# Cross-attention and a snake MoE on one core: steps in an order made offline with a PSUM bank each, the first input in quarters, 64-wide transposes, squares on three engines, slice pairs

## The chip, the cores and the metric

One core of one Trainium2 chip runs the whole program. The metric is the device time of an execution in microseconds (us); a median over several executions is quoted, and the comparisons use runs of the same state (fast). The profile is one execution; its span, from the first to the last instruction, is 1.7 to 2.1 us shorter than the time of the same execution in the thirteen runs where both are on record.

## The reference, cut to what matters

```python
# x (8, 8, 512, 64), state (8, 8, 32, 64); w_in (512, 2048), w_out (2048, 512), alpha (2048)
scores = scale * x @ state.T              # per batch and head: 512 x 32
xread  = softmax(scores) @ state          # 512 token rows
sread  = softmax(scores.T) @ x            # 32 state rows
x2     = concat([xread, sread])           # heads side by side: 8 * 544 rows of 512
h      = x2 @ w_in
g      = h + sin(alpha * h)**2 / (alpha + 1e-9)
out    = g @ w_out                        # 4352 rows of 512, fp32
```

Both kernels fold the state into w_in: M = state @ w_in for each batch, so that h of the token rows is A @ M, with A the normalized weights. The 256 state rows of all batches are done last ("batch 8" below).

## The kernel before

A loop over batches t and over 16 feature blocks f. In each pass it gives a matmul pair for h, some steps of the next batch's attention by a table of slots, the snake (sine, square, gT) two blocks later, and a few output matmuls of the batch before. PSUM has three pools: 4 banks for h, 2 for outputs, 2 for all else.

```python
nc.sync.dma_start(st_nat[:], state...)                 # 512 KB, first in the queue
for k in range(G): nc.sync.dma_start(x_first[...], ...) # batch 0's x in two halves
...
nc.gpsimd.tensor_copy(held[:], st_nat[:, 0, 0:1])      # the weight loads wait for the state
...                                                    # then w_in and w_out by GpSimd's queue

def m_step(b, fs, on_act):                             # one slice of 512 columns of M
    mp = [psX.tile(...) for _ in range(G)]
    for h in range(2):
        for g in range(G):
            for r in range(2):                         # 8 matmuls of 64 rows x 32 columns
                nc.tensor.matmul(mp[g][o0:o0 + Ns, :], stT[rows, ...], w_in_sb[rows, ...])

if f in PLAN[kind(t)]["sq"]: late.append((s2, s, n))   # square on VectorE, one pass later
else: nc.gpsimd.tensor_tensor(s2, s, s, ALU.mult)      # or on GpSimd

# state rows, at the very end: a store writes 4 batches x 32 rows
eng.dma_start(ov[st * n:(st + 1) * n, S:, cols], o_sb[:, cols])
```

The last 128 state rows are two halves of 256 columns, each with its own copy and store.

The softmax here doesn't subtract the row's maximum and nothing guards it: scores larger than these inputs give would overflow.

## Time and profile before

| | |
|---|---|
| time, median of 3 | 240.83 us (239.0 to 241.3) |
| span in the profile | 237.7 us |
| first h matmul, first output matmul | 15.98 us, 25.42 us |
| last matmul ends, tail after it | 230.51 us, 7.2 us |
| busy: TensorE, ScalarE, VectorE, GpSimd | 219.4, 176.9, 171.6, 99.0 us |

How to read it: the span is the start up to the first h matmul, then TensorE's own work with whatever it idles, then the tail. From 61 us on TensorE has no gap of note. Only three things can shorten the span: an earlier start, less idle time or less work between the first h and the last matmul, and a shorter tail. The prediction shows the lines for each.

### The profile page before, as it was taken

To read this page: it belongs to the slowest core of one execution; us is meant where nothing else is said; L and a number is where in the kernel's file an instruction comes from. 1 tells how busy PE (TensorE), PEld (TensorE's weight loads), DVE (VectorE), ACT (ScalarE), POOL (GpSimd) and SP (SyncE) were. 2 spreads that over 40 slices of the span, in tenths; PEclk is the share of its full clock that TensorE was granted. 3 is DMA by queue.
4 is the path that set the end of the run, shared out by engine and by line. 5 is a ranking of instruction groups with operands and counts; after the bars stand their busy time and mean duration, and the time that the engine had idled before them with its cause. 6 is when DMAs were issued, how large, how long until landed. Compare 5 with 4: busy or idle time off the path is not lost.

```text
span 237.7 us, 4198 instructions
## 1 busy us (share of the span) xinstructions
PE 219.4 (92%) x1532; PEld 104.1 (44%) x1532; DVE 171.6 (72%) x321; ACT 176.9 (74%) x277; POOL 99.0 (42%) x107
## 2 busy tenths in 40 slices
PE   6785699898999999999999999999999999999970
PEld 1643233433444344434443444344434444566550
DVE  3569798789878986898689868985889776645300
ACT  3588777889899979997999799969997565554310
POOL 2946494078543354335433544333433356201100
PEclk9999999999999999999999999999999999999997
DMA  6999993913661556075605560540141111111211
GB/s 217 171 196 206 205 156 91 173 48 72 97 148 36 136 97 130 31 138 100 127 31 140 98 126 29 141 112 4 42 132 47 44 45 45 47 44 48 89 21 67
DMA packets 36578, 23.35 MB, mean 98 GB/s; under 512 B 19645, under 2 KB 32205, under 8 KB 36557
## 3 DMA queue, kind: packets, MB, share of 16 engines
q0 software_dynamic: 11504, 7.87, 23.2%
q1 hardware_dynamic: 25020, 15.21, 22.1%
q8 instruction: 12, 0.20, 0.3%
q14 instruction: 10, 0.07, 0.1%
q10 hardware_dynamic: 32, 0.01, 0.1%
HBM read 17.31 MB, written 8.91 MB: 110 GB/s over the span
## 4 chain that ended last, share of the span: by engine, by line
PE 79%; DMA 8%; POOL 4%; issue 2%; ACT 2%; DVE 2%; POOLq 0%
PE o_ps L415 47%; PE h_ps L380 20%; DMA w_out_sb<-in_moe_w_out_dram 6%; PE m_ps L361 4%; PE h_ps L386 3%; DMA st_nat<-in_state_dram 2%; POOL s L396 2%; PE o_ps L440 1%; PE w_ps L316 1%; POOL w_in_sb L159 1%; PE s_ps L271 1%; PE w_ps L327 1%; DVE gT L406 1%; ACT s L391 1%; ACT o_sb L421 0%
## 5 line engine op out<-in xcount | busy, mean ns | idle before, releaser
L415 PE MATMUL o_ps<-w_out_sb,gT 128*128 128x512 bf16 x528 | 135.5, 380 | 2.4 <-DMA w_out_sb<-in_moe_w_out_dram 1.9
L391 ACT ACTIVATE s<-h_ps,alpha_sb 128x512 bf16<-128x512 f32 (+1 forms) x144 | 95.0, 674 | 36.8 <-PE h_ps L380 26.3
L396 POOL TENSOR_TENSOR s<-s 128x512 bf16<-128x512 bf16 (+1 forms) x70 | 71.0, 1021 | 102.0 <-ACT s L391 98.2
L406 DVE SCALAR_TENSOR_TENSOR gT<-s,inva_sb,h_ps 128x512 bf16<-128x512 bf16 (+1 forms) x144 | 98.7, 706 | 15.1 <-POOL s L396 14.3
L380 PE MATMUL h_ps<-AT,M 128*128 128x512 bf16 x256 | 75.5, 379 | 1.9 <-DVE gT L406 1.0
L415 PEld LDWEIGHTS <-gT 128*128 128x128 bf16 x528 | 49.2, 98 | 59.8 <-issue 8.4
L380 PEld LDWEIGHTS <-M 128*128 128x128 bf16 x256 | 24.3, 98 | 31.0 <-issue 4.8
L403 DVE TENSOR_TENSOR s<-s 128x512 bf16<-128x512 bf16 (+1 forms) x74 | 29.0, 411 | 8.5 <-ACT s L391 8.2
L370 ACT CAST M<-m_ps 128x512 bf16<-128x512 f32 x49 | 27.1, 598 | 0.0
L421 ACT COPY o_sb<-o_ps 128x512 f32<-128x512 f32 x33 | 19.3, 588 | 6.1 <-PE o_ps L415 5.1
L284 DVE TENSOR_REDUCE R<-E 128x16 f32<-128x512 bf16 x16 | 10.9, 683 | 14.9 <-ACT E L280 14.9
L280 ACT ACT_TABLE_LOAD x12 | 15.4, 1283 | 0.2
L391 ACT ACT_TABLE_LOAD x12 | 15.4, 1283 | 0.2
L361 PE MATMUL m_ps<-w_in_sb,stT 64*32 64x512 bf16 x256 | 13.7, 393 | 0.2 <-ACT M L370 0.2
L295 POOL TENSOR_TENSOR A<-E,rR 128x512 bf16<-128x512 bf16 x7 | 7.3, 1046 | 15.8 <-DVE rR L285 15.8
L372 DVE CAST M<-m_ps 128x512 bf16<-128x512 f32 x15 | 10.3, 687 | 4.2 <-PE m_ps L361 4.2
L280 ACT ACTIVATE E<-s_ps 128x512 bf16<-128x512 f32 x16 | 9.4, 597 | 3.3 <-PE s_ps L271 3.2
L361 PEld LDWEIGHTS <-stT 64*32 64x32 bf16 x256 | 3.9, 89 | 13.7 <-issue 13.6
L386 PE MATMUL h_ps<-xs_all,w_in_sb 128*128 128x256 bf16 x64 | 9.6, 273 | 0.0
L386 PEld LDWEIGHTS <-w_in_sb 128*128 128x128 bf16 x64 | 6.3, 98 | 4.1
L271 PEld LDWEIGHTS <-xT 128*128 128x128 bf16 x128 | 5.9, 101 | 4.9 <-DVE xT L249 1.8
L336 DVE RECIPROCAL rC<-w_ps 128x128 f32<-128x128 f32 x8 | 7.6, 944 | 0.6 <-PE w_ps L327 0.6
(53 smaller groups left out, 101.0 us busy)
## 6 DMA issues: line engine op xcount, KB each, us to landing
out_dram<-o_sb SPq DMA_DIRECT2D x33, 256.0 KB, 2.3
xnat<-in_x_dram POOLq DMA_DIRECT2D x7, 512.0 KB, 6.8
w_in_sb<-in_moe_w_in_dram POOLq DMA_DIRECT2D x4, 512.0 KB, 9.5
w_out_sb<-in_moe_w_out_dram POOLq DMA_DIRECT2D x4, 512.0 KB, 18.1
x_first<-in_x_dram SPq DMA_DIRECT2D x2, 512.0 KB, 6.2
st_nat<-in_state_dram SPq DMA_DIRECT2D x1, 512.0 KB
out_dram<-o_sb SPq DMA_DIRECT2D x2, 128.0 KB
xT<-xp SPq DMA_TRANSPOSE x6, 3.8
```

The lines of the kernel that those rows point to most:

```text
L280: nc.scalar.activation(a.E[:, g], a.sp[g][:], ACT.Exp, scale=scale)
L284: nc.vector.reduce_sum(a.R[:, g], E8, axis=AX.X)
L361: nc.tensor.matmul(mp[g][o0:o0 + Ns, :], stT[rows, b * G + g, c0:c0 + Ns], w_in_sb[rows, 2 * g + h, fs * FW:(fs + 1) * FW], start=True, st ...
L370: nc.scalar.copy(dst, mp[g][:])
L380: nc.tensor.matmul(hp[:, :n], Ms[t][:, g, f * P:(f + 1) * P], atts[t].AT[:, g, :], start=(g == 0), stop=(g == G - 1),)
L386: nc.tensor.matmul(hp[:, :n], w_in_sb[:, q, f * P:(f + 1) * P], xs_all[:, q, :], start=(q == 0), stop=(q == Q - 1),)
L391: nc.scalar.activation(s[:, :n], hp[:, :n], ACT.Sin, scale=alpha_sb[:, f:f + 1])
L396: nc.gpsimd.tensor_tensor(s2[:, :n], s[:, :n], s[:, :n], ALU.mult)
L403: nc.vector.tensor_tensor(s2[:, :n], s[:, :n], s[:, :n], ALU.mult)
L406: nc.vector.scalar_tensor_tensor(gT[t][:, f, :n], s2[:, :n], inva_sb[:, f:f + 1], hp[:, :n], ALU.mult, ALU.add)
L415: nc.tensor.matmul(op[:], gT[t][:, ft, st * P:(st + 1) * P], w_out_sb[:, ft, :], start=(ft == 0), stop=(ft == FT - 1),)
L421: nc.scalar.copy(o_sb[:], op[:])
```

## The change

The loop and the slot tables are gone. One list of 1336 steps, made offline, gives the program order of everything; each step that needs PSUM names its bank. With it come other changes: batch 0's x in four quarters on two queues and no gate ahead of the weight loads; batch 0's state as a load of its own; transposes that read two heads side by side, 64 columns wide, without a packed copy; squares on GpSimd, ScalarE or VectorE by name; both exp of a batch nearly always side by side; two slices of M in one step from batch 2 on; batch 1's transpose of A by DMA; and another end.

```diff
-PLAN = {0: {'P': (0, 1), ... }}                     # slots by batch and block
+ORDER = """
+lq.0.A lq.1.S consts lq.2.A l_st0 zero.0 ident_ warm_up.6.512.0 zero.1 exp_table lq.3.S l_st
+identf.V li.0 l_alpha xq.0.V li.1 xtq.0.1 xq.1.A li.3 ...
+...                                                 # [cut: some 120 lines]
+""".split()
-    psH = ... bufs=4 ...; psO = ... bufs=2 ...; psX = ... bufs=2 ...
+        k.gpool, k.sinp, k.outp = pool("gpool", 38), pool("sinp", 10), pool("outp", 6)
+        k.banks = [pool(f"bank{i}", 1, space=bass.MemoryType.PSUM) for i in range(8)]
-    held = const.tile([P, 1], FP32, name="held")
-    nc.gpsimd.tensor_copy(held[:], st_nat[:, 0, 0:1])
+    def xt(k, b, g, bank):                           # 64-wide, straight from the load
+        ... k.nc.tensor.transpose(tp[k.half(r), h, ...], k.t["xnat", b][:, 2 * (2 * g + h) + r, ...], ...)
+    def m(k, b, s, *banks):                          # 2 banks: one slice, 4 banks: two
+        for n in range(len(banks) // 2): ...
+    def sq(k, t, f, eng):
+        if eng == "A": k.nc.scalar.activation(s2[:, :n], s[:, :n], ACT.Square)
+        else: k.mul(eng, s2[:, :n], s[:, :n], s[:, :n])
-            eng.dma_start(ov[st * n:(st + 1) * n, S:, cols], o_sb[:, cols])
+            k.nc.sync.dma_start(ov[:, k.S + st::2, cols], o_sb[:, cols])   # 8 batches x 16 rows
+    for step in ORDER:
+        name, *args = step.split(".")
+        getattr(steps, name)(*(int(a) if a.isdigit() else a for a in args))
```

In the list, `h.0.12.2` is h of batch 0, block 12, in bank 2; `si`, `sq`, `gt` are its sine, square and snake; `o.t.st.f0.f1` are output matmuls, `oc` and `os` their copy and store. At the end, the state rows' outputs now come before the last token rows of batch 7.

## The prediction

> **What bounds the kernel now.** I read the page's slices first, then the chain that ended last, then the table of stretches, then the timeline of TensorE, and last the groups by shape for the durations. The slices:
>
> ```profile
> PE   6785699898999999999999999999999999999970
> DVE  3569798789878986898689868985889776645300
> ACT  3588777889899979997999799969997565554310
> GB/s 217 171 196 206 205 156 91 173 48 72 97 148 36 136 97 130 31 138 100 127 31 140 98 126 29 141 112 4 42 132 47 44 45 45 47 44 48 89 21 67
> ```
>
> A slice is 5.9 us. TensorE is full from the eleventh slice to the last but one; before that it is at 5 to 9 tenths, and the bytes are at their highest in the first six slices. The stretches say the same in microseconds:
>
> ```profile
> 18.00:24.00 6.00, 3.16 (x38) 1.74 (x36) 5.87 (x11) 5.14 (x8) 3.52 (x4) 1.00 1.24 206
> 24.00:30.00 6.00, 4.05 (x30) 1.42 (x30) 4.41 (x9) 4.39 (x8) 3.09 (x3) 1.00 1.24 204
> 80.00:100.00 20.00, 20.00 (x145) 9.16 (x144) 15.99 (x31) 17.66 (x27) 8.79 (x9) 1.00 0.46 93
> ```
>
> The columns are TensorE, its weight loads, VectorE, ScalarE and GpSimd in us, then clock, DMA share and GB/s. From 80 to 100 us TensorE never rests, while ScalarE has 2.3 us to spare in 20. From 18 to 24 it rests for 2.8 us of 6.
>
> The chain that ended last, in order of time, at its start and its end:
>
> ```profile
> 0.74 4.39 DMA st_nat<-in_state_dram
> 10.01 15.36 DMA w_out_sb<-in_moe_w_out_dram
> 25.42 1.02 PE o_ps L415 x4
> ...
> 222.69 4.32 PE o_ps L415 x20
> 227.00 3.51 PE o_ps L440 x32
> ```
>
> The state's load gates all weight loads (a GpSimd copy of it stands before them), the first slice of w_out lands at 25.4, and only then can output matmuls start. The last two lines give rates: 4.32/20 = 0.216 us for 512 columns, 3.51/32 = 0.110 for 256. TensorE's last matmul ends at 230.51; the span is 237.7, so the tail (copy, store, end) is 7.2. The first h matmul starts at 15.98 (timeline). Between lie 214.5 us.
>
> How much of that is work? 528 output matmuls x 0.2155 = 113.8; 32 halves x 0.110 = 3.5; 256 h x 0.2155 = 55.2; 64 h of the state rows x 0.1085 = 6.9 (four of them take 0.43 between neighbours). The M step is read here:
>
> ```profile
> 121.52 0.59 PE L380 MATMUL h_ps<-AT,M 128*128 128x512 bf16 x2
> 122.04 0.41 PE L361 MATMUL m_ps<-w_in_sb,stT 64*32 64x512 bf16 x8
> 122.38 1.25 PE L415 MATMUL o_ps<-w_out_sb,gT 128*128 128x512 bf16 x5
> ```
>
> From 121.52 to 122.38 is 0.86; two h matmuls are 0.43, so a slice costs 0.43, twice its 0.215 of streaming. After the first h there are 31 slices = 13.3. Scores 14 x 0.24 = 3.4, the W product 7 x 0.46 = 3.2, the column sums 7 x 0.35 = 2.5 (from starts at 113 to 134 us), transposes of batch 1 about 1.4. Sum 203.2. So 11.3 us of 214.5 are idle, nearly all before 61 us; the chain there runs over the w_out load, gT, ScalarE copies and, from 51 to 60 us, GpSimd squares.
>
> **What the Trainium skill says.** (1) "TensorE: Matmul & The Clock Gate", section "Wait — 56ns, not 53.3ns?": 215.7 ns start to start for 512 columns when warm. The trace agrees (0.216), so this rate can't be improved by an order. (2) "TensorEngine Tiling (Array Packing)", section "Key Properties": changing the tiling mode drains TensorE. The trace agrees: 0.215 beyond streaming per M slice, entered and left from full-array matmuls. (3) "ScalarE: Activation LUTs", section "What ACT_TABLE_LOAD costs": a load is about 1283 ns, an ACTIVATE with immediates 186 ns + 0.833 per element, and neighbours overlap by about 93 ns. The trace has
>
> ```profile
> L391 ACT ACTIVATE s<-h_ps,alpha_sb 128x512 bf16<-128x512 f32 x128 | 87.4, 699 | 27.1 <-PE h_ps L380 26.3 <-POOL A L292 0.2
> L391 ACT ACT_TABLE_LOAD x12 | 15.4, 1283 | 0.2
> L280 ACT ACT_TABLE_LOAD x12 | 15.4, 1283 | 0.2
> ```
>
> and three sines in a row took 1.87, so 0.62 each. The overlap is real, about 0.075. (4) "DMA: Bandwidth & Descriptors", section "Queues, rings and completion order": each DMA engine goes round the queues that have work, packet by packet. No wait of this trace tests it; I use it for the x quarters below.
>
> **The change part by part.** No useful matmul is removed; the order, the banks and the loads change.
>
> Start. The state's load no longer stands before x and the weights. Batch 0's x comes as four 256 KB quarters on two queues, batch 0's state separately as 64 KB, all states in bf16 through GpSimd's queue, which is not gated any more. Before, 1.5 MB were landed at about 8 us (the x cast started at 8.14 without a wait). x and the small state are 1.1 MB; with part of the bandwidth going to the ungated loads I put the last quarter at 6.5. From there, by the order's text and measured durations: cast 0.45, transposes 0.25, copy 0.57, scores 0.3, two exp 1.2 (in part before the last scores), row sums, reciprocals and the normalization on VectorE up to 5.3 after landing, transpose and copy, while ScalarE does sine table 1.5, three stT copies 1.75 and two M copies 1.1. I reach 7.0 after landing, so the first h at 13.5 in place of 16.0: gain 2.5.
>
> Weights. To the first w_out slice GpSimd's queue now reads 0.5 (state) + 3 (w_in) + 1 (x of batch 1) + 1 (w_out) MB, with 1.1 MB on the others: 6.9 MB in 10^6 bytes. Before, 6.3 MB (four w_in, x, one w_out) took from about 6.7 to 25.4: 336 GB/s. At that rate it lands at about 22.5, 3 us earlier. In front of the first output matmuls the new order has 7.8 us of TensorE work (11 h pairs, 4 M slices, the 64-wide transposes), where the old had 4.4 from first h to first output. In the same stretch ScalarE has 9.8 us, or 9.0 with overlap. So idle to the first output, at about 22.8, is near 1.5 in place of 5.0.
>
> Slice pairs. 12 pairs (batches 2 to 7) drain once for two slices: estimate 0.215 + 2 x 0.215 = 0.645 in place of 0.86; 12 x 0.215 = 2.6 saved, all on the path, since TensorE is full there.
>
> 64-wide transposes. They transpose two heads side by side without the packed copy before them and drop the state's doubling (one VectorE and one ScalarE cast, 0.69 and 1.04). TensorE pays about 1.3 for batch 1 in place of 0.9; the wait on the pack before the old transpose (1.44) goes, counted in the idle time. Batch 1's second transpose goes to DMA: 0.5 less on TensorE.
>
> Work after the first h, new: 179.4 (outputs and h) + 6 single slices 2.6 + 12 pairs 7.7 + scores 3.4 + W 3.7 + sums 2.8 + transposes 1.3 = 200.9.
>
> Engines. Squares: 88 GpSimd, 49 ScalarE, 7 VectorE, before 70 and 74 on GpSimd and VectorE. A square on ScalarE is an estimate by the skill's rule: 186 + 427 = 0.61. Counting the order: 49 squares 27.5 on ScalarE; M copies 34 (before 49) and output copies 23 (before 33, and one half) give back about 15; table loads fall from 26 to 16, giving 12.8. So ScalarE stays near 177 busy. From the first h to the scores of batch 5 the sums are TensorE 98.6, ScalarE 104.8 as rows, about 95 with overlap, VectorE 96, GpSimd 63. TensorE still leads, by little. In the last third it leads by 15 and more.
>
> Sum: 13.5 + 200.9 + idle + tail. I allow 5 idle: 1.5 to the first output, 1 to 1.5 up to batch 2's scores (TensorE 20.3, ScalarE 21.2 as rows, VectorE 20.5), 2 in the rest. Tail 7.5: the last copy is whole (0.59 for 0.42) and its store 256 KB, not 128. Span 226.9. The kernel before took 240.83 for a span of 237.7, so 3.1 on top: 230.0. Since an order found offline would close such gaps where it can, I go to 229.5.
>
> **The rivals.** (a) ScalarE becomes the bound. Its stretch to batch 5 is 104.8 without overlap against 98.6; were that the truth, 6 us more idle: about 234. For it: 17.66 busy in 20 even now, and squares come on top in the middle. Against: 10 fewer table loads, overlap seen. (b) Ungated loads slow the x quarters, and the weights still arrive at their own rate: the start gains nothing, +2.5, about 232. For it: the DMA's share is already 0.94 to 1.31 in the first 30 us. (c) The fixed order meets other latencies than it was made for (DMA transposes take 3.8 and 2.7 us, loads up to 18), and a bank held by one late copy stops TensorE, whose queue is in program order: idle stays at 10, about 234 to 237. For it: the chain at 51 to 60 us shows how one late square stalls all; against: 38 gT buffers and 10 for squares leave room. (d) Square on ScalarE needs another table: 49 x one to two loads of 1.28 = 63 to 126 us slower. The page on ScalarE does not say that Square is in the sine's set, but copies between sines reload nothing here; 2 in 100.
>
> **Range and chances.** Zero idle would give 225, idle as before 235.5 or so. 80%: 225 to 235. Faster by over 2% means under 236.0: 0.89; within 2% (rival c in full, or a and b together): 0.08; slower 0.03.
>
> **What would show it.** The first h near 13.5, the first output matmul at 22 to 24; M groups of 16 in a row with 0.64 between their neighbours; 16 table loads; TensorE full from about 40 us; ScalarE busy near 177 and squares of 0.61 there without loads; the last matmul at 218 to 221. Wrong if TensorE shows idle before waits on ScalarE after 60 us (a), the last x cast starts after 8 us (b), or long waits on one bank's copy or a DMA transpose fill the middle (c).

## The result, and the profile after

The changed kernel takes **228.44 us** (228.19 to 228.61, 4 runs) against 240.7 in the same rounds. The ratio is 0.9507, with a 95% interval of 0.9465 to 0.9549. Ratios here are the mean time of one kernel's fast runs over that of the other's fast runs of the same rounds, so not quite the ratio of the medians. The prediction said 229.5 and 225 to 235. The time fell by 12.3 us, the span of the two profiled executions by 11.0: in later rounds, executions of the kernel before with the profiled span (237.6 to 237.8) took 239.6 to 239.8 us, so the profiled one was quicker than the median. All executions of that kernel in later rounds had a mean granted clock of 0.958 to 0.994, the four of the changed kernel 1.0. What follows explains the 11.0.

The slices of the changed kernel (a slice is 5.7 us):

```profile
PE   4599899999999899999999999989999999999993
DVE  3268997998897958888898888798368558782000
ACT  3299988998899899889997599799573789981122
GB/s 175 213 202 206 206 174 55 174 189 123 19 62 127 171 64 0 196 140 85 35 58 229 145 50 0 130 193 5 46 0 154 36 46 49 46 48 3 94 83 102
```

TensorE stands at 8 or 9 tenths from the third slice to the last but one, where before that took until the sixth. But the first two slices are emptier than before: 4 and 5 tenths for 6 and 7. And the last slice has work in it where there was none. The chain of the changed kernel, in order of time, at the start (start, duration, what):

```profile
1.76 8.32 DMA x<-in_x_dram
10.10 0.43 DVE xp L321
...
16.61 1.56 ACT M L467 x3
...
25.38 0.70 DVE gT L514
26.08 0.04 issue
26.12 0.59 PE o_ps L525 x2
```

The last quarter of x, issued at 1.76, takes 8.3 us. The first h matmul, before and after:

```profile
15.98 0.59 PE L380 MATMUL h_ps<-AT,M 128*128 128x512 bf16 x2 [0.72 <-ACT AT L310]
```

```profile
17.25 0.88 PE L484 MATMUL h_ps<-AT,M 128*128 128x512 bf16 x2 [0.21 <-ACT M L467]
```

The first output matmul is at 26.12, after 25.42 before. So the start has become later, not earlier, by 1.3 us. Yet the span is 11.0 shorter. Of the stretch from the first outputs to 61 us this is the line of before and then the line of the changed kernel (TensorE, its weight loads, VectorE, ScalarE, GpSimd busy us with counts, then the clock granted to TensorE as a share of full speed, the busy share of the DMA engines, GB/s):

```profile
25.40:61.30 35.90, 33.39 (x244) 13.52 (x244) 30.90 (x54) 29.03 (x48) 22.18 (x22) 1.00 0.68 125
```

```profile
26.00:61.00 35.00, 34.30 (x221) 15.16 (x225) 31.74 (x55) 31.69 (x50) 21.04 (x21) 1.00 0.72 133
```

Idle time fell from 2.5 to 0.7 us here. (Busy counts a matmul's modelled end too, so true idle is larger in both.) From 60 to 100 us, in the changed kernel:

```profile
60.00:100.00 40.00, 38.86 (x284) 18.14 (x288) 33.40 (x55) 37.06 (x57) 20.16 (x20) 1.00 0.51 106
```

The kernel before had 39.90 busy there. The new order idles for 1.1 us there where the old one idled for 0.1, and it fills the gaps that the old one had early. ScalarE is busy for 93% of this stretch.

The parts of the two spans, by the timeline of TensorE and the counts of the prediction:

| part | before | predicted | measured |
|---|---|---|---|
| start, up to the first h | 15.98 | 13.5 | 17.25 |
| work from there | 203.2 | 200.9 | 200.9 by count |
| idle between | 11.3 | 5 | 4.8 = 222.96 - 17.25 - 200.9 |
| tail after the last matmul | 7.2 | 7.5 | 3.75 = 226.7 - 222.96 |
| span | 237.7 | 226.9 | 226.7 |

The chain at the end of the changed kernel, where the last output matmuls end at 222.96 and the last copy follows:

```profile
220.63 2.34 PE o_ps L525 x10
222.99 0.58 ACT o_sb L533
```

Eleven us are: 1.3 lost at the start, 6.5 won in idle time, 2.3 in work, 3.5 in the tail. Work is counted, so idle time is a remainder and takes up any error of the count. TensorE's busy time in the same two stretches (207.7 of 214.5 us, 201.3 of 205.7) would leave 6.8 and 4.5 us idle, because each matmul before a short gap is drawn longer than its 0.216 us. How the 8.8 us of both terms divide is therefore an estimate. The predicted time is near the measured one because two terms were off by the same 3.75 us in opposite directions. The experiments take these up one by one.

### The profile page after: what moved, and what is told of

Same layout as the page of the kernel before. It is cut to its first block, busy times and chain, and to the rows that moved or that the text cites. A ratio compares the mean times of both kernels' runs of the same rounds, so it can differ in the third digit from the quotient of the medians.

```text
span 226.7 us, 4202 instructions
## 1 busy us (share of the span) xinstructions
PE 212.7 (94%) x1538; PEld 104.6 (46%) x1565; DVE 162.6 (72%) x282; ACT 176.5 (78%) x296; POOL 113.1 (50%) x123
## 4 chain that ended last, share of the span: by engine, by line
PE 65%; DVE 8%; ACT 8%; DMA 7%; POOL 6%; issue 4%; SPq 0%; POOLq 0%; ACTq 0%
PE o_ps L525 41%; PE h_ps L484 13%; POOL s L195 5%; ACT s L498 5%; DMA x<-in_x_dram 4%; DMA xnat<-in_x_dram 4%; DVE gT L514 3%; PE h_ps L490 3%; PE m_ps L459 2%; DVE xp L313 2%; PE s_ps L369 2%; PE w_ps L421 1%; ACT M L467 1%; DVE M L467 1%; PE w_ps L432 1%
## 5 line engine op out<-in xcount | busy, mean ns | idle before, releaser
L525 PE MATMUL o_ps<-w_out_sb,gT 128*128 128x512 bf16 (+1 forms) x540 | 131.6, 373 | 2.1 <-DVE gT L514 0.8
L195 POOL TENSOR_TENSOR s<-s 128x512 bf16<-128x512 bf16 (+1 forms) x88 | 86.2, 997 | 72.2 <-ACT s L498 65.6
L498 ACT ACTIVATE s<-h_ps,alpha_sb 128x512 bf16<-128x512 f32 (+1 forms) x144 | 89.1, 671 | 9.9 <-PE h_ps L484 8.5
L507 ACT ACTIVATE s<-s 128x512 bf16<-128x512 bf16 (+1 forms) x49 | 29.9, 611 | 0.8
L533 ACT COPY o_sb<-o_ps 128x512 f32<-128x512 f32 (+1 forms) x25 | 14.2, 574 | 20.1 <-PE o_ps L525 20.1
L467 ACT CAST M<-m_ps 128x512 bf16<-128x512 f32 x34 | 18.4, 594 | 5.4 <-PE m_ps L459 5.4
L195 POOL TENSOR_TENSOR A<-E,rR 128x512 bf16<-128x512 bf16 x13 | 13.4, 1047 | 17.5 <-DVE rR L386 11.8
L467 DVE CAST M<-m_ps 128x512 bf16<-128x512 f32 x30 | 19.2, 676 | 2.9 <-PE m_ps L459 2.8
L313 DVE COPY xp<-xnat 128x1024 bf16<-128x1024 bf16 x14 | 7.8, 575 | 1.1 <-DMA xnat<-in_x_dram 1.1
L533 DVE COPY o_sb<-o_ps 128x512 f32<-128x512 f32 x10 | 6.9, 686 | 2.3 <-PE o_ps L525 2.1
## 6 DMA issues: line engine op xcount, KB each, us to landing
w_in_sb<-in_moe_w_in_dram POOLq DMA_DIRECT2D x4, 512.0 KB, 12.3
```

The lines of the kernel that those rows point to most:

```text
L195: {"V": k.nc.vector, "G": k.nc.gpsimd}[eng].tensor_tensor(out, a, b, ALU.mult)
L313: k.copy(eng)(k.t["xp", b][:, :, hs, :], k.t["xnat", b][:, hs, :].rearrange("p h (i d) -> p i h d", i=k.C),)
L467: k.copy(eng)(k.t["M", b][:, g, s * k.FW:(s + 1) * k.FW], k.t["m", b, s, g][:])
L498: k.nc.scalar.activation(s[:, :n], k.t["h", t, f][:, :n], ACT.Sin, scale=k.alpha_sb[:, f:f + 1])
L507: k.nc.scalar.activation(s2[:, :n], s[:, :n], ACT.Square)
L525: k.nc.tensor.matmul(k.t["o", t, st, half][:, cols], k.t["gT", t, f][:, rows], k.w_out_sb[:, f, cols], start=(f == 0), stop=(f == k.FT - 1),)
```

## The experiments

Twelve kernels ran, all with the right result. "Changed kernel" is the one with 228.4 us. They ran in later rounds, on two chips, beside the kernel before (medians 240.1 to 240.9) and not beside the changed kernel. So a difference from 228.4 compares rounds, and I take one under 1 us as not resolved. Two runs were slow: one of experiment 1 (234.17) and one of experiment 9 (250.48). The medians quoted take them in; the ratios do not.

### 1. x ahead of the weights

Theory: the weight loads on GpSimd's queue, no longer gated, crowd out the last quarter of x.

```diff
+    def held(k, q):
+        h = k.const.tile([k.P, 1], FP32, name="held")
+        k.nc.gpsimd.tensor_copy(h[:], k.x0[:, 2 * q, 0:1])
-... exp_table lq.3.S l_st identf.V li.0 ...
+... exp_table lq.3.S held.1 l_st identf.V li.0 ...
```

> A GpSimd copy of one element of x's second quarter stands before the state's and the weights' loads, so these start after the first two quarters have landed. Theory (the weight loads on GpSimd's queue crowd out the last quarter, whose cast starts at 10.10 us in the changed kernel): the cast of the last quarter starts at or before 6.8 us, the first h matmul at 13.5 to 14.0 in place of 17.25. If the start sets the end, the time falls by 2.5 to 3.5 us, to about 225.5. Rival 1 (the last quarter is late for its place behind the small state load on its own queue): the cast still starts at 9 us or later and nothing is gained. Rival 2 (the weights set the end of the start): the first h comes early, but the first output matmul waits for w_out or w_in and stays after 25 us, and the time is within 1 us of 228.4.

Measured: 229.98 us, ratio 0.9557, so 1.5 us *longer*. The first part came nearly as expected; this is the timeline of that kernel:

```profile
6.66 0.42 DVE L325 CAST xp<-x 128x512 bf16<-128x512 f32 x1
...
14.24 0.89 PE L488 MATMUL h_ps<-AT,M 128*128 128x512 bf16 x2 [0.21 <-ACT M L471]
...
23.12 0.59 PE L529 MATMUL o_ps<-w_out_sb,gT 128*128 128x512 bf16 x2 [0.35 <-DVE gT L518]
...
36.55 0.59 PE L488 MATMUL h_ps<-AT,M 128*128 128x512 bf16 x2 [2.95 <-DMA AT<-A]
```

The last quarter's cast starts at 6.66 in place of 10.10, 3.4 us earlier; the first h is at 14.24 (expected: 13.5 to 14.0) and the first output matmul at 23.12, both 3.0 us earlier. The bracket in the last line says that TensorE then stood for 2.95 us on the DMA that transposes batch 1's A. Its landing took 6.0 us here, 3.2 in the changed kernel: the weights' queue empties at much the same time as before, near 35 us, and the transpose was now issued in the midst of them (30.5 us in place of 33.5). After that stop the clock of TensorE was at 0.72 from 36 to 42 us. So the contention at the start is shown, and rival 2 was half right: the time was given back, but to a transpose, not to a weight.

### 5. The same, with batch 1's A transposed by TensorE

```diff
-... me.1.2.1.V h.0.8.4 ad.1 h.0.9.2 ...
+... me.1.2.1.V h.0.8.4 h.0.9.2 ...
-... h.0.11.6 si.0.10 gt.0.8 sq.0.9.G ...
+... h.0.11.6 si.0.10 gt.0.8 sq.0.9.G at.1.0.4 at.1.1 ac.1.0.V ac.1.1.A ...
```

> x first as in the first experiment, and batch 1's transpose of A goes over TensorE, a bank and two copies (VectorE and ScalarE), not over DMA. Theory (the 3 us won at the start were lost because that DMA transpose took 6.0 us to land among the weights' loads, with TensorE idle for 3.0 us and its clock lowered after it): no wait over 0.6 us on A's transpose, first output matmul at 23.1, and the time at 225.5 to 226.3, 2 to 3 us under the changed kernel. Rival (the weights' end at about 35 us holds the batch anyway): a wait on w_out, w_in or on batch 2's x of 2 us or more takes its place between 30 and 45 us and the time stays at 228 or above.

Measured: 227.66 us (227.23 to 228.7), ratio 0.9469. The wait on the DMA is gone, and none of 2 us took its place:

```profile
33.27 0.61 PE L405 MATMUL a_ps<-ident,A 128*128 128x128 bf16 x8 [0.35 <-DVE gT L518]
```

It is 2.3 us better than experiment 1, and the intervals of the two ratios do not meet, so the theory stands on the cause. The size was wrong: 0.8 us better than the changed kernel and not 2 to 3, and that 0.8 is not resolved (one of its four runs, 228.7, is above all four of the changed kernel). The h matmul at 29.93 in the changed kernel is at 27.13 here, 2.8 earlier; the W product (the sum over x for the state rows) at 60.99 is at 59.56, 1.4 earlier. In between lie the transposes themselves (0.45), their wait of 0.35, waits of 0.27 and 0.22 behind them, and two more copies on engines that are nearly full there. A start that is 3 us earlier was worth 1.3 us of span in these two executions, 0.8 us of median time.

### 2. Slice pairs undone

Each of the twelve pairs is split; its second slice stands behind the next full-array step.

```diff
-... m.2.0.4.0.6.7 rs.2.1 nm.2.0.0.4.G o.1.1.3.4 ...
+... m.2.0.4.0 rs.2.1 nm.2.0.0.4.G o.1.1.3.4 m.2.1.6.7 ...
```

> The twelve slice pairs are split: the second slice of each stands behind the next full-array step, everything else stays. Theory (each pair saves one entry and exit of the tiled mode, 0.215 us, and TensorE sets the time): 0.43 us between the neighbours of each single slice and 2.6 us longer, 231.0. Rival (the gaps that TensorE has from 60 to 180 us take up the difference): less than 1 us longer.

Measured: 231.04 us (230.47 to 231.17), ratio 0.9603: 2.6 us longer, as expected. In the changed kernel a pair reads:

```profile
52.33 0.38 PE L525 MATMUL o_ps<-w_out_sb,gT 128*128 128x512 bf16 x1
52.64 0.62 PE L459 MATMUL m_ps<-w_in_sb,stT 64*32 64x512 bf16 x16
53.20 1.04 PE L525 MATMUL o_ps<-w_out_sb,gT 128*128 128x512 bf16 x4
```

From 52.33 to 53.20 is 0.87; less the one output matmul of 0.215 it is 0.65 for two slices. Split, in the profile of this experiment:

```profile
51.91 0.41 PE L460 MATMUL m_ps<-w_in_sb,stT 64*32 64x512 bf16 x8
52.25 0.39 PE L526 MATMUL o_ps<-w_out_sb,gT 128*128 128x512 bf16 x1
52.57 0.41 PE L460 MATMUL m_ps<-w_in_sb,stT 64*32 64x512 bf16 x8
52.91 2.33 PE L526 MATMUL o_ps<-w_out_sb,gT 128*128 128x512 bf16 x10
```

From 52.25 to 52.91 is 0.66, so 0.44 for the slice alone. Each tiled group pays about 0.22 us for being entered and left, with one slice in it or with two.

### 3 and 4. The tail

Theory: the tail of 7.2 us before was the landing of state-row stores. "DMA: Bandwidth & Descriptors", section "Why a DMA increments its semaphore by 16 and not by 1", says that a DMA uses the largest number of engines up to 16 that divides the slowest dimension of both sides. With 4 batches as the slowest dimension that would be 4 engines, with 8 batches 8, with 128 token rows 16. Experiment 3 puts the old end into the changed kernel, and experiment 4 puts the new rows into the kernel before.

```diff
 # experiment 3: changed kernel
-k.nc.sync.dma_start(ov[:, k.S + st::2, cols], o_sb[:, cols])
+k.nc.sync.dma_start(ov[4 * st:4 * st + 4, k.S:, cols], o_sb[:, cols])
-... oc.7.1.A os.7.1                                   # oh.8.1.* some 40 steps earlier
+... oc.7.1.A os.7.1 oh.8.1.0.2 och.8.1.0.A osh.8.1.0 oh.8.1.1.3 och.8.1.1.V osh.8.1.1
 # experiment 4: kernel before
-eng.dma_start(ov[st * n:(st + 1) * n, S:, cols], o_sb[:, cols])
+eng.dma_start(ov[:, S + st::2, cols], o_sb[:, cols])
 # [cut: in both, the slices of gT for the matmuls, to match]
```

> The end as before: the two halves of the last 128 state rows are computed, copied and stored after everything else, and state rows go out as 4 batches of 32 rows to a store, not as 8 of 16. Theory (the tail after the last matmul, 7.2 us before and 3.7 now, is the landing of such a store over few DMA engines): the tail is 7 to 7.4 us again and the time 3 to 3.7 us longer, about 231.9. Rival (the tail depends on how full the store queue is, or on the copy's engine): the tail stays under 4.5 us and the time within 0.7 us of 228.4.

> The kernel before with one edit: state rows are stored as 8 batches of 16 rows. Theory (a store's landing goes with the number of DMA engines that share it, 4 with four batches as the slow dimension, 8 with eight): the tail falls from 7.2 to about 5 us and the time by about 2 us. Rival (the place of the store in the queue matters, not its rows): no change within 0.5 us.

Measured: experiment 3 takes 230.22 us (ratio 0.9584), 1.8 longer, with a tail of 4.8 us; experiment 4 takes 238.57 (ratio 0.9914), 1.6 shorter, with a tail of 4.5. The stretches after the last copy, of the kernel before, of experiment 4 and of the changed kernel (only the DMA share and the GB/s at the end matter):

```profile
231.50:236.50 5.00, 0.00 (x0) 0.00 (x0) 0.00 (x0) 0.00 (x0) 0.00 (x0) 0.87 0.24 85
```

```profile
232.00:235.00 3.00, 0.00 (x0) 0.00 (x0) 0.00 (x0) 0.00 (x0) 0.00 (x0) 0.98 0.32 99
```

```profile
223.50:226.00 2.50, 0.00 (x0) 0.00 (x0) 0.00 (x0) 0.07 (x1) 0.00 (x0) 1.00 0.40 156
```

A mean share of 0.24 over five us fits four of sixteen engines that never rest; with token rows it is 0.40. With eight batches the stretch shown has its own pauses; a shorter one gives 0.47, near eight of sixteen:

```profile
231.00:232.50 1.50, 0.45 (x5) 0.16 (x2) 0.42 (x1) 0.00 (x0) 0.00 (x0) 1.00 0.47 160
```

The trace's DMA records say the same: about four packets are in flight at a time at the end of the kernel before, about eight in experiment 4, and up to 16 or 17 while the changed kernel stores token rows. So experiment 4 shows that the rows of the store matter. Its tail fell by 2.7 us and its time by 1.6: in the profiled execution 1.0 us was lost again before 36 us, after a wait of 3.2 us on w_out (1.9 before) and at a clock of 0.91 from 20 to 40 us.

Experiment 3 missed both its theory (7 to 7.4 us of tail) and its rival (under 4.5): it got back only 1.1 of the 3.5 us. What the rest is, no run took alone, but the two traces show a difference in the queue. In the kernel before, the full store of the other 128 state rows and both halves were issued from 227.65 us on, so 512 KB waited for the same few engines; in experiment 3 the full store is out long before, and only the halves, 256 KB, are left. The line of the kernel before, then that of experiment 3:

```profile
229.00:236.00 7.00, 1.50 (x14) 1.09 (x12) 0.42 (x1) 0.20 (x1) 0.00 (x0) 0.94 0.25 73
```

```profile
223.00:227.00 4.00, 0.28 (x3) 0.00 (x0) 0.42 (x1) 0.00 (x0) 0.00 (x0) 0.86 0.22 66
```

73 GB/s for 7 us are 0.51 MB, 66 for 4 us are 0.26 MB: about the same rate, and half the bytes.

### 6 and 10. ScalarE's squares elsewhere

```diff
-... sq.0.15.A ... sq.0.13.A ... (49 squares)
+... sq.0.15.V ... sq.0.13.V ...      # experiment 6; .G in experiment 10
```

> All 49 ScalarE squares on VectorE (0.42 us each there). Theory (the third engine is needed: VectorE's sum to batch 5 is 91 to 96 us against TensorE's 98.6, and some 25 squares more make it 102 to 107): 3 to 7 us longer, TensorE waiting for gT or for copies by VectorE. Rival (TensorE is the bound with slack on all others, and what the third engine took off is spare): within 1 us of 228.4.

> All 49 ScalarE squares on GpSimd (1.05 us each). GpSimd would be busy for 113 + 51 = 164 us of 230. Theory (what counts is the load of the fullest engine): no more than 3 us longer, as GpSimd stays under 75 per cent and ScalarE is relieved by 30 us. Rival (in the stretches where squares come in pairs, a second square of 1.05 us on one engine comes too late for gT, and the PSUM bank of h is held longer): 4 to 12 us longer, with TensorE waiting for gT.

Measured: on VectorE 236.69 us (ratio 0.9848), 8.3 longer and so more than expected; on GpSimd 250.17 (ratio 1.0388), 21.7 longer, slower than the kernel before. My theory for GpSimd is refuted, and the rival's 12 us were too few as well. GpSimd was busy for 160.0 of 249 us, 64%, so it was not full. What TensorE waited for in the first and in the second (total us, times, longest):

```profile
PE h_ps L484 <- DVE gT L514: 5.8, 9, 2.2
```

```profile
PE h_ps L484 <- DVE gT L514: 7.5, 14, 1.1
PE o_ps L525 <- DVE gT L514: 4.3, 4, 2.9
```

And behind it what VectorE waited for, in the changed kernel and in the one with GpSimd's squares:

```profile
DVE gT L514 <- POOL s L195: 12.8, 23, 1.9
```

```profile
DVE gT L514 <- POOL s L195: 33.5, 58, 3.5
```

The bank of h stays taken until gT has read it, and each queue runs in program order. A square that comes later than the order had in mind holds the gT behind it, then the bank, then TensorE. These waits do not add up to 21.7; TensorE is also busy for 220.3 us in place of 212.7 with the same instructions, at a mean clock of 0.973.

Something else delays gT, which the expectations did not have: VectorE's own squares become longer. Durations (least, median, longest, in ns) in the changed kernel, experiment 10 and experiment 6, and one case of experiment 10:

```profile
L195 DVE TENSOR_TENSOR s<-s x7: 418/425/516, 20.7 to 203.2; 128x512 bf16<-128x512 bf16 x7
```

```profile
L195 DVE TENSOR_TENSOR s<-s x7: 417/425/3039, 20.2 to 225.6; 128x512 bf16<-128x512 bf16 x7
```

```profile
L195 DVE TENSOR_TENSOR s<-s x56: 279/425/1210, 19.9 to 213.9; 128x512 bf16<-128x512 bf16 x50, 128x256 bf16<-128x256 bf16 x6
```

```profile
99.03 3.04 DVE L195 TENSOR_TENSOR s<-s 128x512 bf16<-128x512 bf16 x1
99.74 2.04 POOL L195 TENSOR_TENSOR s<-s 128x512 bf16<-128x512 bf16 x2
```

In these traces every 128 x 512 square of VectorE longer than 0.43 us overlapped a tensor operation of GpSimd. Of the 50 in experiment 6, 25 overlapped one and took 0.66 us in the mean; the other 25 took 0.42, the figure that the expectation used for all. In experiment 10 VectorE's packing copies also rose from 575 to 871 ns in the mean; whole gT operations did not (742 and 743). So a square moved to GpSimd also cost VectorE time, and one moved to VectorE took 0.54 us and not 0.42. No run separates this share of the 8.3 and 21.7 us from that of the order.

The order was kept in both experiments: they show what this order needs, not what a new order without ScalarE's squares could reach.

### 7 and 9. Fourteen table loads more

The kernel before had 26 loads of ScalarE's table, the changed one has 16. Experiment 7 adds loads in front of seven exp (the second of six batches, and the first of batch 6, which stood right behind batch 5's), experiment 9 as many a few sines later.

```diff
-... ex.2.0 ... ex.2.1 ...
+... ex.2.0 ... sin_table ex.2.1 ...                  # experiment 7, at seven exp
+... ex.2.0 ... ex.2.1 ... si ... si ... si exp_table sin_table ...   # experiment 9
```

> A one-element sine stands between the two exp of seven batches, so 14 table loads of 1.28 us are added, 18 us of ScalarE time and as many loads as before (30 against 26). Theory of the prediction's rival a (ScalarE is nearly the bound up to batch 5, 95 against 98.6): 4 to 10 us longer with TensorE waiting on ScalarE. Rival (ScalarE's idle time in the order takes them up): under 1.5 us longer.

> Again 14 table loads more (two one-element activations, exp and sine, to each pair), but a few sines after the exp, not between them. Theory (ScalarE's throughput is what counts, 98 per cent taken where TensorE is full): 11 to 17 us longer, as when the loads stood between the exp (15.5). Rival (only the way from scores over exp to A and M is short of time, and loads elsewhere are taken up by ScalarE's queue): under 7 us longer.

Measured: 243.92 us (ratio 1.0148) and 249.55 (ratio 1.0331). Experiment 7 adds 14 x 1.283 + 7 x 0.20 = 19.4 us to ScalarE and 15.5 to the time; experiment 9 adds 20.8 and 21.1. Without its slow run, experiment 9 is at 249.13, so 20.7. So it is not only the way over exp that is short of time: in both places one us of ScalarE's time added 0.8 to 1.0 us. Not all of that is waiting: TensorE's busy time rose too, from 212.7 to 216.0 and 219.4 us, at a mean clock of 0.972 in both profiles. Experiment 9 went past its expected 11 to 17, and why it costs more than experiment 7 was not tested. The stretch from 60 to 100 us of experiment 7:

```profile
60.00:100.00 40.00, 37.18 (x253) 16.80 (x257) 31.06 (x52) 38.80 (x59) 17.41 (x18) 1.00 0.38 82
```

ScalarE now has the 38.80, and TensorE idles. In the changed kernel the two stood at 38.86 for TensorE and 37.06.

### 8. Batch 1 packed, 128 wide

```diff
-... xt.1.0.4 xt.1.1.3 ... pk.1.1.V ... pk.1.0.V ...  # xt reads the load, 64 wide
+... pk.1.0.V pk.1.1.V xt.1.0.4 xt.1.1.3 ...          # xt reads the packed pair
```

> Batch 1's transposes read the packed copy, 128 wide, as before; its two VectorE copies (0.5 us each) stand ahead of them. Theory (the 64-wide form takes the pack off a path that VectorE and TensorE share until 30 us): TensorE waits 0.5 to 1.2 us before these transposes, and the time is 0.5 to 1.2 us longer. Rival (TensorE waits for VectorE and ScalarE there anyway, and the copies only change places): within 0.4 us.

Measured: 229.39 us (228.74 to 231.05), ratio 0.9545. TensorE waits 2.1 us for the packs, yet the time is only 0.9 longer. Two of the four runs had a mean clock of 0.978 and took 231.05 and 229.69; the two with 0.997 and more took 228.74 and 229.09, 0.3 to 0.7 over the changed kernel, all of whose runs had 1.0. The theory's direction holds, its size is not settled.

### 11 and 12. The last tile in halves, and all gains together

```diff
-o.7.1.0.2.4 ... o.7.1.15.16 oc.7.1.A os.7.1
+oh.7.1.0.4 och.7.1.0.A osh.7.1.0 oh.7.1.1.2 och.7.1.1.V osh.7.1.1   # at the end
```

> The last output tile is computed as two halves of 256 columns in two banks, each copied (ScalarE, VectorE) and stored by itself, all else as in the changed kernel. Theory (only the last half's copy and landing stand in the tail): 0.3 to 0.7 us shorter. Rival (two stores of 1 KB runs land no sooner than one of 2 KB runs): within 0.2 us.

> x first, batch 1's A over TensorE, and the split last tile together. If the gains add (0.8 and 0.3 to 0.7): 226.9 to 227.4. Rival (they share the same slack): no better than 227.6.

Measured over five rounds: 228.34 us (227.53 to 230.19), ratio 0.9497, for the split alone; 227.57 (227.22 to 229.01), ratio 0.9466, for both. The tails are 3.3 and 3.4 us for 3.75, so the expected mechanism is seen at 0.35 to 0.45 us, but the time does not resolve it: no better than the changed kernel alone and than experiment 5. At 227.57 the sum of gains falls between its theory (to 227.4) and its rival (from 227.6). The best kernel is this last one, 0.9 us (0.4%) under the changed kernel; the intervals of the two ratios overlap, so that lead is likely, not proved.

## Why the prediction was right, by its own steps

- **What bounds the kernel.** Right. TensorE's work and its idle time set the time: the work counted to 200.9 us, and the pairs cost 2.6 us when undone, as counted.
- **Slice pairs.** Right in size: 0.65 us measured, 0.645 predicted.
- **The start.** Wrong. The step that failed is "I put the last quarter at 6.5". It was 10.1. The prediction had seen that the loads share the engines packet by packet, named the slower start as rival (b) and gave it +2.5 us; the truth was +3.75. By its own sign for (b), a last cast after 8 us, that rival came true. From the quarter's cast to the first h it gave 7.0 us, and 17.25 - 10.10 = 7.15 were measured, so the chain was right and only its beginning was late. Experiment 1 shows the cause: with the weights and states gated behind the second quarter the cast is at 6.66.
- **Weights.** The first output matmul was put at 22.8 and came at 26.12, with no wait on a weight; the first slice of w_out landed at 22.05 (issued at 5.25, 16.8 to landing), against the predicted 22.5. The stretch from first h to first output was put at 9.3 and measured 8.9; it was late only because it began late.
- **The tail.** Wrong. The step is "Tail 7.5: the last copy is whole ... and its store 256 KB, not 128". It took the bytes of the store to be what counts. It was 3.75: the last store is token rows over more engines, and the state rows are out earlier. The prediction had the moved end in front of it and did not ask why the old tail was 7.2 us when stores landed in 2.3 at the median. Its sign for the last matmul, 218 to 221, failed with the start: it ended at 222.96.
- **Span to time.** "so 3.1 on top" compared a median with the span of one faster run. The same execution's difference is 1.7.
- **Idle time.** Right by the same count: 5 allowed, 4.8 left over, of which 1.1 (8.87 - 7.8) up to the first output, with 1.5 predicted.
- **ScalarE's load.** Right in the sum: 16 table loads, 176.5 us busy for 177. The squares in it were too small, 27.5 us for 29.9 measured (0.638 us each and not 0.61), so other terms were too large by about as much. The statement that TensorE leads "by little" was borne out by experiments 7 and 9: one us more of ScalarE's time cost 0.8 to 1.0 us. Rival (a) did not come true in the changed kernel, but it is near.
- **Rival (c)**, an order that meets other latencies: not in the changed kernel, where TensorE's waits from 60 to 180 us are below 1 us each. It is what happened in experiment 1, and in part in 6 and 10, as soon as one latency was changed under a fixed order.
- **Rival (d)**, a table load for each square: refuted by the 16 loads.

The sum as measured: 17.25 + 200.9 + 4.8 + 3.75 + 1.7 = 228.4. The sum as predicted: 13.5 + 200.9 + 5 + 7.5 + 3.1 = 230.0, with 0.5 taken off. The range was right for a reason that the sum did not fully deserve: start and tail cancelled.

What stays open: the offline order can't be taken away alone, since banks, pairs and squares are named in it. That it brought most of the 6.5 us of idle time is argued from the stretches, not shown by a run. What ScalarE's 49 squares are worth under an order made without them is open too.

## What to carry to other kernels

Once a core has its fullest engine at 97% and the next at 93%, look for each term of the sum, start, idle, work and tail, by itself, and test it by itself: two wrong terms can make a right total. A fixed order makes the latencies it was made for part of the program: an earlier load was worth nothing here until a step that met its old latency was changed too (experiments 1 and 5). Before work is moved to an engine with idle time, look at how long the same instruction takes when both engines are busy. Look at the last store: the number of DMA engines that share it was worth 1.6 us by itself, and rows and place together 1.8 us, against 2.6 for twelve saved drains.

## What the Trainium skill lacked or had wrong

- "TensorEngine Tiling (Array Packing)", "Key Properties": it says that a change of mode drains the array but not what that costs. Here it is 0.22 us per tiled group of 8 or 16 matmuls, entered from and left to full-array matmuls.
- "DMA: Bandwidth & Descriptors", "Queues, rings and completion order": the round between queues is stated, its effect is not sized. A 256 KB quarter issued at 1.76 us was used at 10.10 with the weights' loads beside it and at 6.66 with them held back; a DMA transpose took 6.0 us to land in place of 3.2.
- The same page, the passage on how many engines a DMA uses: the runs agree with it (mean share 0.24 where it gives 4 of 16), but it does not warn that a store at a kernel's end pays for it: 7.2 us of tail, 4.5 with eight batches as the slow dimension, 3.75 with token rows last.
- "ScalarE: Activation LUTs", "Table sets: the hidden batching unit": it does not say whether Square can run beside Sin. 49 squares among the sines caused no load: 16 in all, none of them on the line of the squares. By the rule of the same page's section "What ACT_TABLE_LOAD costs", an ACTIVATE with immediates takes 186 ns + 0.833 per element, an estimate of 0.61 us for 512; the 43 squares of 128 x 512 took 0.638 us in the mean.
